# Partial sums written into another PSUM bank by ScalarE, a residual seeded in PSUM, and a reordered start, in a four-block fp16 kernel

## The chip, the cores and the metric

The kernel runs on one core of one Trainium2 chip. The metric is the device time of one execution in microseconds (us), lower is better. A "ratio" below is the mean time of one kernel's fast runs over the mean of the other's fast runs of the same rounds, so it is not quite the ratio of the medians that are quoted beside it.

## The reference, cut to what matters

```python
x = x + A(layernorm(x))   # linear attention, 32 heads of 32, then @ wo
x = x + B(layernorm(x))   # h = (n @ w_gate) * (n @ w_up);  h @ w_down
x = x + A(layernorm(x))
x = x + B(layernorm(x))   # S = 2048 tokens, D = 1024, F = 3584
```

## The kernel before

Every engine has one instruction stream, and a recording helper adds semaphores from the declared reads and writes: `rd`/`wr` for SBUF ranges, `prd`/`pwr` for PSUM banks. The matrix products of block B use a seven-product (Strassen-Winograd) scheme on 2x2 blocks, so a "unit" of gate/up is seven products of four 128x512 matmuls. Gate/up runs four times (two layers, two halves of the tokens), 28 units each; I call each such run a pass. A down stage follows each pass. In the first pass DVE also makes weight combinations that the later passes read back.

The unit of gate/up (cuts marked ...; DVE is VectorE; `stt` is a DVE multiply-add, or with `op1` a multiply, that reads PSUM, `tt` a DVE operation on two inputs; a "product" is one of the seven, `pe("1", ...)` to `pe("7", ...)`):

```python
X, Y, Z = B_GX[u % 2], B_GY[u % 2], B_GZ        # Z: one bank for all units
def cp(i, bank):                                # ScalarE: PSUM -> SBUF
    P.add("act", lambda e: e.activation(tm[i][0], psb(bank), AF.Copy, scale=SG), prd=[bank], wr=tm[i][1])
def fin(b, bank, ti):
    ...
    if ti is None:
        if m == 0:   # gate: ScalarE evicts; up: one DVE multiply
            P.add("act", lambda e: e.activation(g4[b], psb(bank), AF.Copy, scale=SG), prd=[bank], wr=gr)
        else:
            stt(hv[:, j, :], psb(bank), SG, g4[b], gr, hr, prd=[bank], op1=ALU.mult)
    elif m == 0:
        stt(g4[b], psb(bank), SG, tm[ti][0], tm[ti][1], gr, prd=[bank])
    else:            # two DVE operations
        stt(ut, psb(bank), SG, tm[ti][0], tm[ti][1], ur, prd=[bank])
        tt(hv[:, j, :], ut, g4[b], ALU.mult, ur + gr, hr)
def part1():
    pe("1", X, True); cp(0, X)
    pe("2", Z, True); fin(0, Z, 0)
...
# order: 1 2 | 4 of the unit before | 6 | 3 of the unit before | 5 7
```

The end of block A, here the "y stage": sixteen token tiles, two halves each. ScalarE also computes the next layernorm's output in it, and `norm` still runs for two tiles.

```python
def y_grp(i, dh, n):
    ...  # eight matmuls into one of four banks
    if dh == 0:
        P.add("dve", lambda e: e.tensor_tensor(out=xs, in0=psb(bank), in1=xs, op=ALU.add), ...)
        return
    P.add("act", lambda e: e.copy(ysb[yb], psb(bank)), ...)
    P.add("pool", lambda e: e.tensor_tensor(out=xs, in0=xs, in1=ysb[yb], op=ALU.add), ...)
...
O_P = [O_ZACC, RE]                          # buffers of norm
O_YS = [RE + i * 2048 for i in range(2)]    # ysb: the same memory as the second of them
```

The w_down weights are prepared by DVE in 14 "ticks" in the first pass: `if ... wdn[0] * 24 <= u * NJ` with `NJ = 14`. A tick prepares what the tick before it asked to load into a single buffer, and asks for the next.

Of the kernel before, what the change touches and what calls it, by code (L numbers as in the profile page):

```python
# [180 lines left out]
def build_kernel(nc, A_x, A_wqkv, A_wo, B_w_gate, B_w_up, B_w_down, out):  # L181
    _, S, D = A_x.shape
    F = B_w_gate.shape[1]
    NST, NSB, KT, NG, NFT, NDH = S // 128, S // 512, D // 128, D // 128, F // 128, D // 512
    NJ = NFT // 2
# [5 lines left out]
    NHOLD = 2  # L191
# [95 lines left out]
    with ExitStack() as es:  # L287
# [54 lines left out]
        def psb(b):  # L342
            return ps[:, b, :]
# [23 lines left out]
        def R(o, n):  # L367
            return [(o, o + n)]

        def r_x(i, lo=0, hi=D):  # L370
            return [(O_X + (i * D + lo) * 2, O_X + (i * D + hi) * 2)]
# [7 lines left out]
        def r_xT(s0, s1):  # L379
            return _seg(O_XT, KT, S * 2, s0 * 2, s1 * 2)  # L380

        def r_w(base, lo, hi):
            return _seg(base, KT, D * 2, lo * 2, hi * 2)
# [4 lines left out]
        def mset(ap, v, rng):  # L388
            P.add("pool", lambda e: e.memset(ap, v), wr=rng)

        mset(ones, 1.0, R(O_ONES, 256))
        mset(mhalf, -0.5, R(O_MHALF, 4))
        mset(mask, 0.0, R(O_MASK, 256))
# [38 lines left out]
        class LN:  # L432
# [59 lines left out]
            def transpose(self, n):  # L492
                d, r = self.dst(n)
                i = self.order[n]
                if self.use_dma:
                    P.add("sp", lambda e: e.dma_start_transpose(xnT[:, :, i * 128:(i + 1) * 128], d),
                          rd=r, wr=r_xT(i * 128, (i + 1) * 128), dma_sem=KTF[i] if self.to == "A0" else KTL[n % 2])
                    return
                tp = psb_h(B_TP)[:, 0:KT * 128].rearrange("p (k s) -> p k s", s=128)

                def fn(e):
                    return [e.transpose(tp[:, k, :], d[:, k * 128:(k + 1) * 128], ident) for k in range(KT)]
                P.add("pe", fn, rd=r + R(O_IDENT, 256), pwr=[B_TP])
                P.add("act", lambda e: e.copy(xnT[:, :, i * 128:(i + 1) * 128], tp), prd=[B_TP], wr=r_xT(i * 128, (i + 1) * 128))  # L504
# [66 lines left out]
        def ring_issue():  # L571
            n = RG["n"]
            if n >= 2 * NPASS:
                return
            RG["n"] = n + 1
            o = r_slot(n)[0][0]
            ps_, u = divmod(n, NPASS)
            sl = (n + 1) % NR
            if u < NU:
                j, m = divmod(u, 2)  # L580
                raw = vb(o, 2048).rearrange("p (k c) -> p k c", c=256)
                dma(raw, wgu_v[m][:, :, j * 256:(j + 1) * 256], r_slot(n, 0, 4096), KRR[sl])
                if not (RG["first"] and ps_ == 0):
                    dma(vh(o + 4096, 2048), sscr[u], r_slot(n, 4096, 8192), KRS[sl], rd=R(V_S + u * 32, 32))
                return
            q, hf = divmod(u - NU, 2)
            q = DPROD[q]
            js = slice(hf * 7, hf * 7 + 7)
            if q in "123":
                e, d = {"1": (0, 0), "2": (1, 0), "3": (1, 1)}[q]  # L590
                dma(vb(o, 7 * 512).rearrange("p (j c) -> p j c", c=512), wd_v[:, js, e, d * 512:(d + 1) * 512], r_slot(n, 0, 7168), KRR[sl])
            else:
                t = {"5": 0, "6": 1, "7": 2, "4": 3}[q]
                dma(vh(o, 7 * 512).rearrange("p (j c) -> p j c", c=512), tscr[t][:, js, :], r_slot(n, 0, 7168), KRR[sl],
                    rd=R(V_D + hf * 7 * 32, 7 * 32))
# [55 lines left out]
        def layer_A(lnp, nxt, first):  # L651
# [52 lines left out]
            if first:  # L704
                lnp.start(0)
                lnp.b_one()
                lnp.step_t(1)
                lnp.start(1)
                lnp.b_one()
                lnp.start(2)  # L710
            else:
                lnp.use_dma = True
            seq = [("k", i) for i in range(NHOLD)]
            for i in range(NHOLD, NST):
                seq += [("k", i), ("q", i - NHOLD)]
            for kind, i in seq:
                for h in range(2):
                    if kind == "k":
# [96 lines left out]
                wprod(NG + g, [0, 2, 1, 3][g - 4], g % 2 == 0)  # L815
            proj_q(*held[3])()

            def y_grp(i, dh, n):
                bank = B_YY[(2 * n + dh) % 4]

                def fn(e):
                    return [e.matmul(psb(bank), xnT[:, g, i * 128:(i + 1) * 128], wp[:, g, dh * 512:(dh + 1) * 512],  # L822
                                     start=(g == 0), stop=(g == NG - 1)) for g in range(NG)]
                P.add("pe", fn, rd=r_xT(i * 128, (i + 1) * 128) + r_w(O_WP, dh * 512, (dh + 1) * 512), pwr=[bank])
                xs = x_res[:, i, dh * 512:(dh + 1) * 512]
                rx = r_x(i, dh * 512, (dh + 1) * 512)
                if dh == 0:
                    P.add("dve", lambda e: e.tensor_tensor(out=xs, in0=psb(bank), in1=xs, op=ALU.add), prd=[bank], rd=rx, wr=rx)
                    return
                yb = n % 2  # L830
                P.add("act", lambda e: e.copy(ysb[yb], psb(bank)), prd=[bank], wr=R(O_YS[yb], 2048))  # L831
                P.add("pool", lambda e: e.tensor_tensor(out=xs, in0=xs, in1=ysb[yb], op=ALU.add), rd=rx + R(O_YS[yb], 2048), wr=rx)  # L832

            nxt.use_dma = True
            nxt.on_act = YACT
            ring_begin(first)
            for _ in range(3):
                ring_issue()
            for i in range(NST):
                if na[0] < NST:  # L840
                    if i % 3 == 2:
                        norm(tok[na[0]])
                        na[0] += 1
                elif RG["n"] < NR:
                    ring_issue()
                nxt.step_t(1)
                nxt.b1_one()
                if i >= 2:
                    nxt.start(i - 2)
                y_grp(tok[i], 0, i)  # L850
                nxt.b2_one()
                y_grp(tok[i], 1, i)
                if nxt.t_next >= 8 and RG["tq"] is None:
                    RG["tq"] = t_ops(0)
                if RG["tq"]:
                    RG["tq"].pop(0)()
# [3 lines left out]
        def layer_B(lnp, nxt, first):  # L860
# [10 lines left out]
            def unit(ps_, u):  # L871
# [43 lines left out]
                        stt(ut, psb(bank), SG, tm[ti][0], tm[ti][1], ur, prd=[bank])  # L915
                        tt(hv[:, j, :], ut, g4[b], ALU.mult, ur + gr, hr)

                def part1():
                    pe("1", X, True)
                    cp(0, X)  # L920
                    pe("2", Z, True)
                    fin(0, Z, 0)

                def part_p4():
                    pe("4", X, False)
                    fin(2, X, None)

                def part2():
                    pe("6", X, False)
                    cp(1, X)  # L930

# [1 line left out]
                    pe("3", Y, False)  # L933
                    fin(3, Y, 1)

                def part3():
                    pe("5", Y, True)
                    pe("7", X, False)
                    cp(2, X)
                    fin(1, Y, 2)  # L940
                return part1, part_p4, part2, part_p3, part3

            def gateup(ps_, ticks):
                prev = None
                jit = first and ps_ == 0
                for u in range(NU):
                    n = ps_ * NPASS + u
                    cur = unit(ps_, u)
                    if jit and u == 0:
                        prep_s(n)  # L950
                        prep_s(n + 1)
                    cur[0]()
                    if prev:
                        prev[1]()
                    cur[2]()
                    if prev:
                        prev[3]()
                        ring_issue()
                    cur[4]()
                    if jit:  # L960
                        store_s(n)
                        if u + 2 < NU:
                            prep_s(n + 2)
                    ticks(u)
                    prev = cur
                def tail():
                    prev[1]()
                    prev[3]()
                    ring_issue()
                return tail  # L970
# [95 lines left out]
            def ticks0(u):  # L1066
                if not lnp.done():
                    lnp.flush_step()
                if first and wdn[0] < NJ and wdn[0] * 24 <= u * NJ:
                    wd_tick(1)  # L1070
                    wd_tick(0)

# [45 lines left out]
        dh0 = D // 2  # L1118
        dma(x_res[:, 0, 0:dh0], x2[0:128, 0:dh0], r_x(0, 0, dh0), KX[0])
        dma(x_res[:, 0, dh0:D], x2[0:128, dh0:D], r_x(0, dh0, D), KXB)  # L1120
        wq_ = [("k", 0), ("k", 1), ("q", 0), ("q", 1)]
        for i in range(1, NST):
            if wq_ and (i <= NDH or i >= 3):
                load_w(*wq_.pop(0))
            dma(x_res[:, i, :], x2[i * 128:(i + 1) * 128, :], r_x(i), KX[i])

        O_WRM = O_A[0]
        wrm = vh(O_WRM, 512)
        mset(wrm, 0.0, R(O_WRM, 1024))
        P.add("pe", lambda e: [e.matmul(psb(B_KVT[1]), ident, wrm, start=True, stop=True) for _ in range(PE_WARM)],  # L1130
              rd=R(O_IDENT, 256) + R(O_WRM, 1024), pwr=[B_KVT[1]])
        nat = list(range(NST))
        alt = [4, 5, 6, 7, 0, 1, 2, 3, 12, 13, 14, 15, 8, 9, 10, 11]
        lnA = LN("A0", nat)
# [45 lines left out]
```

## Time and profile before

| | before |
|---|---|
| device time, median of 3 | 1507.83 us (1507.47 to 1508.62) |
| TensorE (PE) busy | 98% of the span |
| DVE / ScalarE / GpSimd busy | 65% / 27% / 17% |

The first part of the page gives, for each engine, its busy time, share and number of instructions (PEld is PE's weight loads, ACT ScalarE, POOL GpSimd):

```profile
PE 1481.8 (98%) x6925; PEld 673.9 (45%) x6990; DVE 974.0 (65%) x1642; ACT 400.1 (27%) x643; POOL 257.9 (17%) x271
```

PE is the bound, and its matmuls cannot become fewer in this change. What remains is its idle time. This is PE's own part of the view of waits (who waited for whom: total us, times, longest):

```profile
PE ps L822 <- ACT arena L831: 4.9, 5, 2.1
PE ps L894 <- DVE arena L601: 4.8, 4, 1.6
PE ps L660 <- ACT arena L504: 3.4, 3, 1.1
PE ps L1130 <- POOL arena L389: 3.3, 1, 3.3
PE ps L894 <- DVE arena L598: 1.8, 1, 1.8
...
```

L822 is the y stage, L894 gate/up, L660 the projections, L1130 the warm-up matmuls, L1006 the down stage. The timeline of PE places the waits (start, length, operation, count, and in brackets the idle time before it and who ended it):

```profile
9.19 1.90 PE L660 MATMUL ps<-arena 128*128 128x512 bf16 x8 [1.10 <-ACT arena L504]
11.38 1.90 PE L660 MATMUL ps<-arena 128*128 128x512 bf16 x8 [0.28 <-DMA arena<-in_A_wqkv_dram]
...
20.09 3.63 PE L660 MATMUL ps<-arena 128*128 128x512 bf16 x16 [1.15 <-ACT arena L504]
...
219.15 3.40 PE L822 MATMUL ps<-arena 128*128 128x512 bf16 x15 [1.09 <-ACT arena L831]
...
249.92 15.04 PE L894 MATMUL ps<-arena 128*128 128x512 f16 x68 [1.81 <-DVE arena L598]
266.38 36.43 PE L894 MATMUL ps<-arena 128*128 128x512 f16 x168 [1.42 <-DVE arena L601]
304.23 31.53 PE L894 MATMUL ps<-arena 128*128 128x512 f16 x144 [1.42 <-DVE arena L601]
...
379.29 42.75 PE L894 MATMUL ps<-arena 128*128 128x512 f16 x196 [1.55 <-DVE arena L601]
...
972.19 24.43 PE L822 MATMUL ps<-arena 128*128 128x512 bf16 x102 [2.07 <-ACT arena L831]
```

The rows left out show no other long stall (a second one of 1.15 us in the head, one of 0.36 at 336.13 us, and a few in the y stages). Three passes of gate/up and all down stages have none. So the change can win in the head, in the two y stages (188.08 to 246.22 us and 935.79 to 996.45 us, ScalarE busy 23.47 in each), and in the first pass (246.22 to 422.10 us, DVE busy 143.73).

### The profile page before, as it was taken

To read this page: it belongs to the slowest core of one execution; us is meant where nothing else is said; L and a number is where in the kernel's file an instruction comes from. 1 tells how busy PE (TensorE), PEld (TensorE's weight loads), DVE (VectorE), ACT (ScalarE), POOL (GpSimd) and SP (SyncE) were. 2 spreads that over 40 slices of the span, in tenths; PEclk is the share of its full clock that TensorE was granted. 3 is DMA by queue.
4 is the path that set the end of the run, shared out by engine and by line. 5 is a ranking of instruction groups with operands and counts; after the bars stand their busy time and mean duration, and the time that the engine had idled before them with its cause. 6 is when DMAs were issued, how large, how long until landed. Compare 5 with 4: busy or idle time off the path is not lost.

```text
span 1507.3 us, 17881 instructions
## 1 busy us (share of the span) xinstructions
PE 1481.8 (98%) x6925; PEld 673.9 (45%) x6990; DVE 974.0 (65%) x1642; ACT 400.1 (27%) x643; POOL 257.9 (17%) x271
## 2 busy tenths in 40 slices
PE   8999999999999999999999999999999999999999
PEld 3444444444444444444444444344444444444444
DVE  7986869888856475455488778675455554544553
ACT  3332334333300133330023313343333002333200
POOL 4543644000000010000034345540000000000000
PEclk9999999999999999999999999999999999999999
DMA  6134655988764697644465247656654456555452
GB/s 223 36 91 109 151 125 111 283 262 271 240 224 159 226 257 201 174 162 143 136 195 170 88 102 175 145 120 188 177 172 157 164 189 196 168 176 177 136 172 100
DMA packets 300644, 254.41 MB, mean 169 GB/s; under 512 B 102288, under 2 KB 266384, under 8 KB 300560
## 3 DMA queue, kind: packets, MB, share of 16 engines
q1 hardware_dynamic: 300560, 253.27, 58.4%
q8 instruction: 55, 0.90, 0.3%
q14 instruction: 29, 0.24, 0.0%
HBM read 195.04 MB, written 34.60 MB: 152 GB/s over the span
## 4 chain that ended last, share of the span: by engine, by line
PE 87%; DVE 6%; DMA 3%; POOL 2%; issue 1%; ACT 1%; SPq 0%; POOLq 0%; DVEq 0%; ACTq 0%
PE ps L894 42%; PE ps L1006 22%; PE ps L660 14%; PE ps L741 6%; PE ps L822 2%; DVE arena L598 1%; DMA arena<-arena 1%; DMA arena<-in_B_w_down_dram 1%; DVE arena L408 1%; DVE arena L683 1%; DVE arena L680 1%; POOL arena L689 1%; DMA arena<-in_A_wqkv_dram 1%; DVE arena L601 1%; PE ps L753 0%
## 5 line engine op out<-in xcount | busy, mean ns | idle before, releaser
L894 PE MATMUL ps<-arena 128*128 128x512 f16 x3136 | 679.9, 379 | 6.6 <-DVE arena L601 4.8
L601 DVE SCALAR_TENSOR_TENSOR arena<-ps,arena 128x512 f16<-128x512 f32 (+2 forms) x536 | 364.6, 689 | 415.9 <-PE ps L1006 154.6
L894 PEld LDWEIGHTS ps<-arena 128*128 128x128 f16 (+1 forms) x3136 | 305.4, 98 | 379.8 <-DVE arena L601 9.1
L898 ACT ACTIVATE arena<-ps 128x512 f32<-128x512 f32 x336 | 200.6, 597 | 552.8 <-PE ps L894 549.4
L1006 PE MATMUL ps<-arena 128*128 128x512 f16 (+1 forms) x1548 | 338.0, 379 | 1.1
L1006 PEld LDWEIGHTS ps<-arena 128*128 128x128 f16 x1568 | 153.5, 98 | 185.0
L598 DVE TENSOR_TENSOR arena<-arena 128x512 f16<-128x512 f16 (+3 forms) x416 | 222.7, 557 | 12.2 <-DMA arena<-in_B_w_down_dram 5.0
L660 PE MATMUL ps<-arena 128*128 128x512 bf16 x1003 | 222.4, 379 | 4.8 <-ACT arena L504 3.4
L660 PEld LDWEIGHTS ps<-arena 128*128 128x128 f16 x1024 | 99.6, 98 | 122.7 <-ACT arena L504 3.9
L546 ACT ACTIVATE arena<-ps 128x512 f32<-128x512 f32 x128 | 76.4, 597 | 232.8 <-PE ps L660 217.1
L822 PE MATMUL ps<-arena 128*128 128x512 bf16 x502 | 113.2, 383 | 6.0 <-ACT arena L831 4.9
L411 POOL TENSOR_SCALAR arena<-arena 128x1 f32<-128x1 f32 x64 | 20.7, 324 | 553.3 <-DVE arena L410 553.3
L741 PE MATMUL ps<-arena 128*128 128x512 bf16 x499 | 114.2, 379 | 0.6
L408 DVE BATCH_NORM_STATS2 arena<-arena 128x6 f32<-128x512 bf16 x128 | 88.2, 689 | 8.8 <-DMA arena<-in_A_x_dram 6.6
L549 DVE SCALAR_TENSOR_TENSOR arena<-ps,arena 128x512 bf16<-128x512 f32 x128 | 88.5, 692 | 4.4
L689 POOL TENSOR_TENSOR arena<-arena 128x1024 f16<-128x1024 f32 x32 | 80.2, 2507 | 60.5 <-DVE arena L687 51.0
L672 POOL TENSOR_TENSOR arena<-arena 128x512 f32<-128x512 f32 x60 | 74.6, 1248 | 88.4 <-DVE arena L549 87.0
L547 DVE TENSOR_SCALAR arena<-arena 128x512 f32<-128x512 f32 x128 | 65.6, 513 | 29.5 <-ACT arena L546 28.3
L822 PEld LDWEIGHTS ps<-arena 128*128 128x128 f16 x512 | 49.8, 99 | 69.0 <-ACT arena L831 7.6
L741 PEld LDWEIGHTS ps<-arena 128*128 128x128 f16 x512 | 49.2, 98 | 55.7
L908 ACT ACTIVATE arena<-ps 128x512 f16<-128x512 f32 x56 | 33.4, 597 | 63.3 <-PE ps L894 63.3
L832 POOL TENSOR_TENSOR arena<-arena 128x512 bf16<-128x512 bf16 x32 | 42.1, 1316 | 44.2 <-ACT arena L831 44.2
(41 smaller groups left out, 362.5 us busy)
## 6 DMA issues: line engine op xcount, KB each, us to landing
arena<-s_scratch SPq DMA_DIRECT2D x84, 512.0 KB, 4.4
arena<-in_B_w_gate_dram SPq DMA_DIRECT2D x56, 512.0 KB, 3.9
arena<-in_B_w_up_dram SPq DMA_DIRECT2D x56, 512.0 KB, 4.0
arena<-t_scratch SPq DMA_DIRECT2D x32, 896.0 KB, 4.8
arena<-in_B_w_down_dram SPq DMA_DIRECT2D x24, 896.0 KB, 4.7
s_scratch<-arena SPq DMA_DIRECT2D x28, 512.0 KB, 7.1
arena<-in_A_wqkv_dram SPq DMA_DIRECT2D x12, 1024.0 KB, 8.6
arena<-in_A_x_dram SPq DMA_DIRECT2D x31, 256.0 KB, 4.9
```

Of the source, the lines that this page charges most:

```text
L408: P.add("dve", (lambda h: lambda e: e.bn_stats(st[j][:, 6 * h:6 * h + 6], x_res[:, i, (D // 2) * h:(D // 2) * (h + 1)]))(h), rd=r_x(i, (D ...
L546: P.add("act", lambda e: e.activation(etmp[r], psb(bank), AF.Exp), prd=[bank], wr=er)
L549: P.add("dve", lambda e: e.scalar_tensor_tensor(out=dst_ap, in0=psb(bank), scalar=0.0, in1=etmp[r], op0=ALU.max, op1=ALU.add), prd=[bank], ...
L598: P.add("dve", lambda e: e.tensor_tensor(out=out, in0=a, in1=b, op=op), rd=rd, wr=wr, prd=prd)
L601: P.add("dve", lambda e: e.scalar_tensor_tensor(out=out, in0=a, scalar=sc, in1=b, op0=ALU.mult, op1=op1), rd=rd, wr=wr, prd=prd)
L660: return [e.matmul(psb(bank), xnT[:, k, i * 128:(i + 1) * 128], w[:, k, h * 512:(h + 1) * 512], start=(k == 0), stop=(k == KT - 1)) for k ...
L689: P.add("pool", lambda e: e.tensor_tensor(out=asb[b].rearrange("p (h c) -> p h c", c=32), in0=pbuf.rearrange("p (h c) -> p h c", c=32), in ...
L741: return [e.matmul(psb(bank), xr[:, t, j * 128:(j + 1) * 128], pk[:, h, t, :], start=(t == 0), stop=(t == NST - 1)) for t in range(NST)]
L822: return [e.matmul(psb(bank), xnT[:, g, i * 128:(i + 1) * 128], wp[:, g, dh * 512:(dh + 1) * 512], start=(g == 0), stop=(g == NG - 1)) for ...
L894: P.add("pe", lambda e: [e.matmul(psb(bank), w[:, k, :], x[:, k, :], start=(start and k == 0), stop=(k == 3), skip_group_check=True) for k ...
L898: P.add("act", lambda e: e.activation(tm[i][0], psb(bank), AF.Copy, scale=SG), prd=[bank], wr=tm[i][1])
L1006: return [e.matmul(psb(bank), hv[:, 7 * hf + k, t * 128:(t + 1) * 128], w[:, k, :], start=(start and hf == 0 and k == 0), stop=(hf == 1 an ...
```

## The change

Its intent is to take work off DVE and GpSimd. (a) In gate/up, ScalarE copies product 1 from bank X to bank Z, and product 2 accumulates on top, so that DVE need not add the two. To give the copy time, product 4 of the unit before goes between 1 and 2. (b) The w_down ticks start three units later and follow each other faster. (c) In the y stage, ScalarE puts the residual of the second half into PSUM ahead of the matmuls, and the GpSimd add goes. (d) In the head, the warm-up no longer waits for the identity matrix, the first transpose is evicted in two halves, and query i precedes key i+2. The diff, cut:

```diff
+        P.add("pe", lambda e: [e.matmul(psb(B_KVT[1]), wrm[:, 0:128], wrm, ...) for _ in range(PE_WARM)], ...)   # now first
...
+                if self.to == "A0" and n == 0:     # first transpose in two halves, two copies
...
-                seq += [("k", i), ("q", i - NHOLD)]
+                pair = [("k", i), ("q", i - NHOLD)]
+                seq += pair[::-1] if first and i < NPE_T else pair
...
+            def y_seed(n):
+                    xs, bank = x_res[:, tok[n], 512:1024], B_YY[(2 * n + 1) % 4]
+                    P.add("act", lambda e: e.copy(psb(bank), xs), rd=r_x(tok[n], 512, 1024), pwr=[bank])
...
-                                     start=(g == 0), stop=(g == NG - 1)) for g in range(NG)]
+                                     start=(dh == 0 and g == 0), stop=(g == NG - 1), skip_group_check=True) for g in range(NG)]
...
-                P.add("act", lambda e: e.copy(ysb[yb], psb(bank)), prd=[bank], wr=R(O_YS[yb], 2048))
-                P.add("pool", lambda e: e.tensor_tensor(out=xs, in0=xs, in1=ysb[yb], op=ALU.add), ...)
+                P.add("act", lambda e: e.copy(xs, psb(bank)), prd=[bank], wr=rx)
...
-                def part1():
+                def part_p1():
                     pe("1", X, True)
-                    cp(0, X)
-                    pe("2", Z, True)
-                    fin(0, Z, 0)
+                    P.add("act", lambda e: e.copy(psb(Z), psb(X)), prd=[X], pwr=[Z])
...
+                def part_p26():
+                    pe("2", Z, False)
+                    fin(0, Z, None)
...  # order now: 1 | 4 of the unit before | 2 6 | 3 of the unit before | 5 7; unit 0: 1 5 2 6, 1 of unit 1, 7
-                if first and wdn[0] < NJ and wdn[0] * 24 <= u * NJ:
+                if first and wdn[0] < NJ and wdn[0] * 22 <= (u - 3) * NJ:
```

The rewritten list of first loads issues the same loads in the same order as before.

More of the change, by code (lines that the diff above doesn't have):

```diff
@@ L389, in mset @@
             P.add("pool", lambda e: e.memset(ap, v), wr=rng)
+        wrm = vh(O_A[0], 512)
+        mset(wrm, 0.0, R(O_A[0], 1024))
+        P.add("pe", lambda e: [e.matmul(psb(B_KVT[1]), wrm[:, 0:128], wrm, start=True, stop=True) for _ in range(PE_WARM)],
+              rd=R(O_A[0], 1024), pwr=[B_KVT[1]])
         mset(ones, 1.0, R(O_ONES, 256))
@@ L497, in transpose @@
                           rd=r, wr=r_xT(i * 128, (i + 1) * 128), dma_sem=KTF[i] if self.to == "A0" else KTL[n % 2])
+                    return
+                if self.to == "A0" and n == 0:
+                    for hf, b in enumerate((B_TP, B_KQ[3])):
+                        tq_ = psb_h(b)[:, 0:512].rearrange("p (k s) -> p k s", s=128)
+                        P.add("pe", (lambda hf, tq_: lambda e: [e.transpose(tq_[:, k, :], d[:, (4 * hf + k) * 128:(4 * hf + k + 1) * 128], ident) for k in range(4)])(hf, tq_),
+                              rd=r + R(O_IDENT, 256), pwr=[b])
+                        P.add("act", (lambda hf, tq_: lambda e: e.copy(xnT[:, 4 * hf:4 * hf + 4, i * 128:(i + 1) * 128], tq_))(hf, tq_),
+                              prd=[b], wr=_seg(O_XT + 4 * hf * S * 2, 4, S * 2, i * 256, (i + 1) * 256))
                     return
@@ L706, in layer_A @@
                 lnp.b_one()
+                lnp.start(1)
                 lnp.step_t(1)
-                lnp.start(1)
                 lnp.b_one()
@@ L816, in layer_A @@
             proj_q(*held[3])()
+            def y_seed(n):
+                if n < NST:
+                    xs, bank = x_res[:, tok[n], 512:1024], B_YY[(2 * n + 1) % 4]
+                    P.add("act", lambda e: e.copy(psb(bank), xs), rd=r_x(tok[n], 512, 1024), pwr=[bank])
             def y_grp(i, dh, n):
@@ L822, in fn @@
                     return [e.matmul(psb(bank), xnT[:, g, i * 128:(i + 1) * 128], wp[:, g, dh * 512:(dh + 1) * 512],
-                                     start=(g == 0), stop=(g == NG - 1)) for g in range(NG)]
-                P.add("pe", fn, rd=r_xT(i * 128, (i + 1) * 128) + r_w(O_WP, dh * 512, (dh + 1) * 512), pwr=[bank])
+                                     start=(dh == 0 and g == 0), stop=(g == NG - 1), skip_group_check=True) for g in range(NG)]
                 xs = x_res[:, i, dh * 512:(dh + 1) * 512]
                 rx = r_x(i, dh * 512, (dh + 1) * 512)
+                P.add("pe", fn, rd=r_xT(i * 128, (i + 1) * 128) + r_w(O_WP, dh * 512, (dh + 1) * 512), pwr=[bank])
                 if dh == 0:
@@ L829, in y_grp @@
                     return
-                yb = n % 2
-                P.add("act", lambda e: e.copy(ysb[yb], psb(bank)), prd=[bank], wr=R(O_YS[yb], 2048))
-                P.add("pool", lambda e: e.tensor_tensor(out=xs, in0=xs, in1=ysb[yb], op=ALU.add), rd=rx + R(O_YS[yb], 2048), wr=rx)
+                P.add("act", lambda e: e.copy(xs, psb(bank)), prd=[bank], wr=rx)
             nxt.use_dma = True
@@ L838, in layer_A @@
                 ring_issue()
+            y_seed(0)
             for i in range(NST):
@@ L850, in layer_A @@
                 y_grp(tok[i], 0, i)
+                y_seed(i + 1)
                 nxt.b2_one()
@@ L926, in part_p4 @@
                     fin(2, X, None)
-                def part2():
+                def part_p26():
+                    pe("2", Z, False)
+                    fin(0, Z, None)
                     pe("6", X, False)
@@ L934, in part_p3, with part_p5, part_p7 @@
                     fin(3, Y, 1)
-                def part3():
+                def part_p5():
                     pe("5", Y, True)
+                def part_p7():
                     pe("7", X, False)
@@ L940, in part3 @@
                     fin(1, Y, 2)
-                return part1, part_p4, part2, part_p3, part3
+                return part_p1, part_p4, part_p26, part_p3, part_p5, part_p7
             def gateup(ps_, ticks):
@@ L945, in gateup @@
                 jit = first and ps_ == 0
+                units = [unit(ps_, u) for u in range(NU)]
                 for u in range(NU):
                     n = ps_ * NPASS + u
-                    cur = unit(ps_, u)
+                    cur = units[u]
                     if jit and u == 0:
@@ L951, in gateup @@
                         prep_s(n + 1)
-                    cur[0]()
+                    if u != 1:
+                        cur[0]()
+                    if u == 1:
+                        cur[4]()
                     if prev:
                         prev[1]()
-                    cur[2]()
-                    if prev:
+                        cur[2]()
                         prev[3]()
                         ring_issue()
-                    cur[4]()
+                        if u != 1:
+                            cur[4]()
+                    else:
+                        cur[4]()
+                        cur[2]()
+                        units[1][0]()
+                    cur[5]()
                     if jit:
@@ L1120, in build_kernel, with xload @@
         dma(x_res[:, 0, dh0:D], x2[0:128, dh0:D], r_x(0, dh0, D), KXB)
-        wq_ = [("k", 0), ("k", 1), ("q", 0), ("q", 1)]
-        for i in range(1, NST):
-            if wq_ and (i <= NDH or i >= 3):
-                load_w(*wq_.pop(0))
+        def xload(i):
             dma(x_res[:, i, :], x2[i * 128:(i + 1) * 128, :], r_x(i), KX[i])
-        O_WRM = O_A[0]
-        wrm = vh(O_WRM, 512)
-        mset(wrm, 0.0, R(O_WRM, 1024))
-        P.add("pe", lambda e: [e.matmul(psb(B_KVT[1]), ident, wrm, start=True, stop=True) for _ in range(PE_WARM)],
-              rd=R(O_IDENT, 256) + R(O_WRM, 1024), pwr=[B_KVT[1]])
+        load_w("k", 0)
+        xload(1)
+        load_w("k", 1)
+        xload(2)
+        load_w("q", 0)
+        xload(3)
+        load_w("q", 1)
+        for i in range(4, NST):
+            xload(i)
         nat = list(range(NST))
```

## The prediction

> **What bounds it now.** TensorE. The page gives PE 98% busy. The timeline shows 512-column matmuls 0.216 us apart; the change leaves their number unchanged (112 gate/up units of seven products of four). So only PE idle time can be won. The waits view of PE adds up to about 19 us:
> - head, first 25 us: 3.3 waiting for the warm-up's memset, 1.1 + 1.15 + 1.15 for the ScalarE copy of a transpose, 0.3 for a weight load;
> - residual (y) stages: 2.4 in layer 1, 3.1 in layer 2;
> - first gate/up pass (246-422 us): 6.6. There DVE is busy 144 of 176 us. Three of its five stalls (1.42, 0.36, 1.55) follow a DVE wait for a w_down load;
> - other gate/up and down passes: none.
>
> **Change, costed.**
> 1. *Gate/up.* Per pair of units DVE loses one 0.69 us multiply-add from PSUM and one 0.42 us multiply; ScalarE gains one 0.60 us eviction: about 1.1 us of DVE per 12.1 us pair. Only the first pass has stalls to give. The w_down preparation starts three units later, missing the layernorm work that I blame for the stall at 266 us (1.42). It has five back-to-back ticks against three, but after each the bank that PE needs is one DVE operation away, not two: 0.7 us less per stall. In unit 0, product 5 before 2 costs 0.5 us. Net 6.6 -> about 3.5.
>    New risk: product 2 waits for the copy of product 1 with one product (0.864 us) in between, and product 4 likewise for the eviction of 7. From the trace: ScalarE starts 0.20 us after PE's next issue, 0.585 (a copy) or 0.597 (an activation), 0.055 to PE: 0.84-0.85 us. It just fits; I allow +1 us in all. The Trainium skill, "ScalarE: Activation LUTs"[...], calls PSUM ScalarE's faster destination; this trace has no such copy.
> 2. *y stage.* 32 GpSimd adds of 1.3 us go; 32 seeds of about 0.56 us come on ScalarE, which has room (23.5 of 58 us busy). Half 1 still waits for a layernorm activation two tokens back, now plus a seed. But DVE's wait of 2.0 us for a GpSimd add at 207 us (shared buffer) goes, and what follows comes 2 us earlier. 2.4 + 3.1 -> about 2.3.
>    The seed is added only where the accumulate bits stand: the Trainium skill, "PSUM — Partial Sum Buffer", rule 2, says ScalarE writes leave them, and a matmul without the first flag adds where they are set. Earlier full-bank matmuls set them: I expect correct results.
> 3. *Head.* Warm-up starts at 1.4 us instead of 3.3, but the second key weight half lands at 11.33 us and the load order is unchanged, so that buys nothing. Query 0 before key 2 hides one transpose copy: -1.3 us.
>
> **Sum.** 1507.8 - 1.3 - 3.2 - 3.1 + 1.0 = **1501.2 us**, 8 in 10 between **1496.5 and 1507.5**. Faster by over 2%: 0.01; within: 0.97; slower: 0.02.
>
> **What would show it.** Timeline: second projection still at 11.4 us; no stall before query 0. Waits: GpSimd residual adds gone; y stalls more than halved; first pass stalls 3-4 us. Windows: DVE down about 14 us per gate/up pass, PE unchanged.
>
> **What would make it wrong.** The tight hand-over missing by 0.05 us a unit (+5 us or more); the clock falling back in the idle head (+2 us); more w_down waits reaching PE; or the y stages losing all stalls (-2 us).

## More of the kernel before

The busy times in the first y stage, the first pass, the second y stage, and in one short stretch of the latter (the columns are window, length, busy time of each engine with instruction counts, granted clock, DMA share, GB/s):

```profile
188.08:246.22 58.14, 55.51 (x252) 24.65 (x256) 43.15 (x83) 23.47 (x29) 33.01 (x43) 1.00 0.58 115
246.22:422.10 175.88, 169.23 (x778) 75.07 (x778) 143.73 (x316) 59.20 (x100) 4.21 (x8) 1.00 0.83 248
935.79:996.45 60.66, 57.31 (x252) 25.16 (x256) 42.95 (x83) 23.47 (x29) 33.01 (x43) 0.97 0.64 152
973.40:976.81 3.41, 3.41 (x10) 1.21 (x8) 2.28 (x5) 1.13 (x1) 0.72 (x2) 0.50 0.54 122
```

I did not read the last row before predicting. It matters below: 1.2 us after the end of the stall of 2.07 us (PE goes on at 972.19 us) the clock granted to PE falls to 0.50 for 3.41 us.

## The result, and the profile after

| | before | after |
|---|---|---|
| device time, median of 4 each | 1507.69 us | 1497.39 us (1496.84 to 1497.64) |
| ratio, 95% interval | | 0.993 (0.9913 to 0.9947) |
| span of the trace | 1507.3 us | 1495.1 us |

The outputs are correct, so the matmuls did add to what ScalarE had put into PSUM, as the prediction expected from the page that it names. The time is 3.8 us below the predicted 1501.2 and inside the range. The page's engine line after:

```profile
PE 1479.0 (99%) x6925; PEld 660.1 (44%) x6990; DVE 913.9 (61%) x1530; ACT 449.2 (30%) x732; POOL 216.0 (14%) x239
```

DVE lost 60 us and GpSimd 42, ScalarE gained 49; the number of matmuls is the same. PE's waits after (L840 is the y stage, L912 gate/up, L672 the projections, L938 the copy between banks, L834 the seed):

```profile
PE ps L840 <- ACT ps L834: 2.7, 3, 1.4
PE ps L672 <- DMA arena<-in_A_wqkv_dram: 1.6, 1, 1.6
PE ps L393 <- POOL arena L389: 1.4, 1, 1.4
PE ps L912 <- DVE arena L613: 1.3, 2, 0.9
...
PE ps L912 <- ACT ps L938: 0.6, 1, 0.6
...
```

And the timeline of PE after:

```profile
7.91 1.90 PE L672 MATMUL ps<-arena 128*128 128x512 bf16 x8 [0.74 <-ACT arena L508]
11.41 1.90 PE L672 MATMUL ps<-arena 128*128 128x512 bf16 x8 [1.60 <-DMA arena<-in_A_wqkv_dram]
...
18.82 7.07 PE L672 MATMUL ps<-arena 128*128 128x512 bf16 x32
...
220.69 22.62 PE L840 MATMUL ps<-arena 128*128 128x512 bf16 x102 [0.92 <-ACT ps L834]
243.15 77.12 PE L912 MATMUL ps<-arena 128*128 128x512 f16 x356
320.62 48.78 PE L912 MATMUL ps<-arena 128*128 128x512 f16 x224 [0.35 <-DVE arena L613]
370.33 42.48 PE L912 MATMUL ps<-arena 128*128 128x512 f16 x196 [0.93 <-DVE arena L613]
...
960.75 3.63 PE L840 MATMUL ps<-arena 128*128 128x512 bf16 x16 [1.44 <-ACT ps L834]
```

The second projection starts at 11.41 us as before (11.38): the warm-up starts earlier, and PE then waits for a weight load. The first pass starts with no stall and has two small ones. The windows of the same three stages:

```profile
186.80:243.15 56.35, 55.16 (x253) 24.96 (x257) 44.25 (x86) 33.78 (x45) 14.04 (x29) 1.00 0.58 122
243.15:412.86 169.71, 168.29 (x777) 72.12 (x777) 127.53 (x285) 66.11 (x113) 2.33 (x6) 1.00 0.83 254
926.35:983.68 57.33, 55.33 (x252) 24.87 (x256) 42.42 (x82) 32.14 (x44) 14.01 (x28) 1.00 0.62 160
```

From one stage's first matmul to the next stage's, the traces differ by: projections -1.3 us, first y stage -1.8, first pass -6.2, second y stage -3.3, the pass after it +0.6 (a new wait for the copy), the rest -0.2. The sum is -12.2 us, the difference of the two spans. The medians differ by less, 10.3 us, and the fall of the clock is most of the reason. Of 27 runs of the kernel before, 17 have a mean granted clock of 1.000 (median 1507.25 us) and ten one of 0.998 or 0.999 (1507.96 to 1511.10 us). The profiled run of the kernel before is one of the latter kind (0.999, 1509.03 us): its second y stage shows some 1.7 us that most runs, and so the median, do not have.

Two rows of the traces explain more than the rest. First, the start of the first pass in the kernel before, where PE waited 1.81 us (timeline of all engines in a window of 1.2 us):

```profile
248.34 1.16 POOL L832 TENSOR_TENSOR arena<-arena 128x512 bf16<-128x512 bf16 x1
248.34 1.43 DVE L598 TENSOR_TENSOR arena<-arena 128x512 f16<-128x512 f16 x1
```

The DVE operation is the second of eight that prepare the first two units, and product 6 of the first needs its result. It took 1.43 us; its seven neighbours took 0.41 to 0.43 us. A GpSimd residual add ran from the same moment for 1.16 us. The Trainium skill, "SBUF — State Buffer", section "Who interferes with whom", says that a DVE instruction with two SBUF inputs contends with a GpSimd instruction that reads SBUF, that the shared port pair is an exclusive lock, and that the issue order decides who blocks. The trace agrees, roughly: waiting out 1.16 us and then a normal 0.42 would be 1.6, and 1.43 were seen. The opposite order is in the same trace, where the DVE operation came first and the add took 1.79 us:

```profile
237.72 1.22 DVE L598 TENSOR_TENSOR arena<-arena 128x2048 f16<-128x2048 f16 x1
238.17 1.79 POOL L832 TENSOR_TENSOR arena<-arena 128x512 bf16<-128x512 bf16 x1
```

So it was with all eight of the 32 adds that began while such a DVE operation on two SBUF inputs ran (1.74 to 1.79 us). The other 24 took 1.16 or 1.17, also those that ran beside DVE operations with only one input in SBUF.

Second, the wait inside the first y stage of the kernel before (timeline; L680 is `norm` on the second buffer, which shares its memory with `ysb`):

```profile
206.21 1.16 POOL L832 TENSOR_TENSOR arena<-arena 128x512 bf16<-128x512 bf16 x1 [0.38 <-ACT arena L831]
207.41 1.23 DVE L680 TENSOR_TENSOR arena<-arena 128x1024 f32<-128x1024 bf16 x1 [1.98 <-POOL arena L832]
```

### The profile page after: what moved, and what is told of

It is laid out like the page before. It is cut to its first block, busy times and chain, and to the rows that moved or that the text cites. A ratio compares the mean times of both kernels' runs of the same rounds, so it can differ in the third digit from the quotient of the medians.

```text
span 1495.1 us, 17704 instructions
## 1 busy us (share of the span) xinstructions
PE 1479.0 (99%) x6925; PEld 660.1 (44%) x6990; DVE 913.9 (61%) x1530; ACT 449.2 (30%) x732; POOL 216.0 (14%) x239
## 3 DMA queue, kind: packets, MB, share of 16 engines
q1 hardware_dynamic: 300560, 253.27, 57.4%
## 4 chain that ended last, share of the span: by engine, by line
PE 91%; DVE 3%; DMA 3%; issue 1%; POOL 1%; ACT 1%; SPq 0%; ACTq 0%
PE ps L912 43%; PE ps L1035 23%; PE ps L672 15%; PE ps L754 7%; PE ps L840 2%; DMA arena<-in_B_w_down_dram 1%; DVE arena L610 1%; DVE arena L412 1%; DMA arena<-arena 1%; DMA arena<-in_A_wqkv_dram 1%; POOL arena L701 1%; PE ps L766 0%; PE ps L794 0%; SPq L386 0%; POOL arena L417 0%
## 5 line engine op out<-in xcount | busy, mean ns | idle before, releaser
L912 PE MATMUL ps<-arena 128*128 128x512 f16 x3136 | 679.0, 379 | 1.9 <-DVE arena L613 1.3
L613 DVE SCALAR_TENSOR_TENSOR arena<-ps,arena 128x512 f16<-128x512 f32 (+2 forms) x480 | 327.2, 689 | 470.6 <-PE ps L912 161.8
L912 PEld LDWEIGHTS ps<-arena 128*128 128x128 f16 (+1 forms) x3136 | 291.4, 98 | 388.2 <-ACT arena L916 36.0
L672 PE MATMUL ps<-arena 128*128 128x512 bf16 x1003 | 222.1, 379 | 4.6 <-DMA arena<-in_A_wqkv_dram 1.6
L916 ACT ACTIVATE arena<-ps 128x512 f32<-128x512 f32 x224 | 133.7, 597 | 291.1 <-PE ps L912 288.9
L610 DVE TENSOR_TENSOR arena<-arena 128x512 f16<-128x512 f16 (+3 forms) x360 | 197.9, 574 | 18.3 <-DMA arena<-in_B_w_down_dram 8.3
L672 PEld LDWEIGHTS ps<-arena 128*128 128x128 f16 x1024 | 99.6, 98 | 122.4 <-DMA arena<-in_A_wqkv_dram 2.1
L558 ACT ACTIVATE arena<-ps 128x512 f32<-128x512 f32 x128 | 76.4, 597 | 232.6 <-PE ps L672 218.4
L938 ACT COPY ps<-ps 128x512 f32<-128x512 f32 x112 | 63.9, 570 | 204.3 <-PE ps L912 203.7
L840 PE MATMUL ps<-arena 128*128 128x512 bf16 x502 | 110.8, 379 | 3.2 <-ACT ps L834 2.7
L926 ACT ACTIVATE arena<-ps 128x512 f16<-128x512 f32 x112 | 66.9, 597 | 84.5 <-PE ps L912 84.5
L840 PEld LDWEIGHTS ps<-arena 128*128 128x128 f16 x512 | 49.8, 98 | 63.9 <-ACT ps L834 4.4
L754 PEld LDWEIGHTS ps<-arena 128*128 128x128 f16 x512 | 49.3, 98 | 55.7
```

The source lines that it names most:

```text
L558: P.add("act", lambda e: e.activation(etmp[r], psb(bank), AF.Exp), prd=[bank], wr=er)
L610: P.add("dve", lambda e: e.tensor_tensor(out=out, in0=a, in1=b, op=op), rd=rd, wr=wr, prd=prd)
L613: P.add("dve", lambda e: e.scalar_tensor_tensor(out=out, in0=a, scalar=sc, in1=b, op0=ALU.mult, op1=op1), rd=rd, wr=wr, prd=prd)
L672: return [e.matmul(psb(bank), xnT[:, k, i * 128:(i + 1) * 128], w[:, k, h * 512:(h + 1) * 512], start=(k == 0), stop=(k == KT - 1)) for k ...
L754: return [e.matmul(psb(bank), xr[:, t, j * 128:(j + 1) * 128], pk[:, h, t, :], start=(t == 0), stop=(t == NST - 1)) for t in range(NST)]
L840: return [e.matmul(psb(bank), xnT[:, g, i * 128:(i + 1) * 128], wp[:, g, dh * 512:(dh + 1) * 512], start=(dh == 0 and g == 0), stop=(g == ...
```

## The experiments

Twelve kernels ran. All outputs were correct. The median of the kernel before was 1508.12, 1507.84 and 1507.41 us in the three calls; the changed kernel did not run in them, so I compare with its ratio, 0.993, and with its trace. Times by stage from the traces (first matmul to the next stage's first matmul, the projections from the start of the span; us; one trace each):

| kernel | projections | y stage 1 | first pass | y stage 2 | median, ratio (95%) |
|---|---|---|---|---|---|
| before | 118.1 | 58.1 | 175.9 | 60.7 | |
| after | 116.9 | 56.4 | 169.7 | 57.3 | 1497.39, 0.9930 (0.9913-0.9947) |
| e1_head | 117.0 | 57.7 | 174.7 | 63.1 | 1506.63, 0.9988 (0.9976-1.0001) |
| e2_y | 117.6 | 56.3 | 173.8 | 59.1 | 1502.69, 0.9961 (0.9949-0.9974) |
| e3_gu | 118.2 | 57.8 | 172.0 | 60.5 | 1502.97, 0.9965 (0.9953-0.9978) |
| e4_ysb | 117.7 | 55.8 | 174.6 | 58.8 | 1503.46, 0.9965 (0.9952-0.9979) |
| e5_oldtick | 116.2 | 56.7 | 171.9 | 57.4 | 1498.07, 0.9933 (0.9920-0.9945) |
| e6_p1sbuf | 117.0 | 56.5 | 170.2 | 58.9 | 1498.20, 0.9937 (0.9924-0.9949) |
| e7_adjacent | 116.3 | 57.0 | 189.4 | 58.9 | 1582.69, 1.0496 (1.0481-1.0510) |
| e8_spaced | 116.6 | 56.4 | 169.8 | 57.7 | 1496.49, 0.9923 (0.9910-0.9937) |
| e9_yorder | | | | | 1494.48 (3 fast runs), 0.9909 (0.9894-0.9925) |
| e10_headT | 115.5 | 57.0 | 170.2 | 57.5 | 1496.08, 0.9920 (0.9906-0.9933) |
| e11_latewarm | 116.8 | 56.6 | 170.3 | 57.3 | 1496.69, 0.9923 (0.9911-0.9935) |
| e12_best | 115.4 | 55.3 | 169.3 | 55.7 | 1492.79, 0.9898 (0.9885-0.9912) |

Stages that are the same code differ between traces by up to 2.6 us in the second y stage (60.5 in e3_gu, 63.1 in e1_head), 1.2 in the first pass (174.6 in e4_ysb, 175.9 before) and 0.8 in the others. A difference of one trace below that is not an argument by itself.

### e1_head: only the start

The kernel before with the hunks of the diff that concern the head, and nothing else.

> Only the head of the change (early warm-up, first transpose in two halves, query 0 before key 2). My theory: the second key weight half still lands at 11.3 us, so the early warm-up gives nothing, and one hidden transpose copy gives 1.3 us: the stage after the projections starts 1.3 us earlier (116.85 us), all later stages as before, 1506.4 us. Rival: the 1.9 us that the warm-up starts earlier are won too: 3 us or more.

The projections are 1.2 us shorter in the trace, as expected, and the second projection waits 1.6 us for its weights. The time ratio does not exclude 1 (0.9976 to 1.0001). Two of the five runs have a clock of 0.998, the profiled one among them: there a stall of 3.7 us in the second y stage was followed by 6.8 us at half clock. Among runs with a clock of 1.000, the median is 1506.20 us of three, against 1507.67 of five of the kernel before. The rival (3 us or more) is excluded for the stage, less firmly for the time.

### e2_y: only the y stage

The kernel before with `y_seed` and the new `y_grp`.

> Only the y stage of the change (seed in PSUM, no GpSimd add). My theory: 1.8 us from the first y stage and about 2.7 from the second; and, because in the kernel before a GpSimd add ran at the same time as the second of the eight preparation operations of DVE at the start of the first gate/up pass (1.43 us in place of 0.42), that operation takes 0.42 us here and the first gate/up stall falls from 1.8 us to under 0.5. Sum -5 to -6.5 us, about 1502. Rival: the stall at the start of gate/up belongs to the order of the products, and stays at 1.8: -4.5 at most.

-1.9 and -1.6 us in the y stages, -2.1 in the first pass, median 1502.69: as expected in sum. In the first pass the GpSimd add is gone, and the same preparation operation now merges with the next in the timeline, two in 0.76 us:

```profile
245.63 0.76 DVE L598 TENSOR_TENSOR arena<-arena 128x512 f16<-128x512 f16 x2
```

The stall at the start, with the old order of products, is the one before this row of PE:

```profile
246.20 15.03 PE L899 MATMUL ps<-arena 128*128 128x512 f16 x68 [0.33 <-DVE arena L598]
```

It fell from 1.81 to 0.33 us. The rival falls. The second y stage is another matter: its stalls are 1.92 and 1.54 us, more than the 3.1 before, and no half clock followed them. In this trace the seed did not shorten them; the 1.6 us are about what the half clock had cost.

### e3_gu: only gate/up

The kernel before with the copy between banks, the new order and the new ticks.

> Only the gate/up part of the change (product 1 copied between PSUM banks, order, later w_down ticks). My theory: y stages unchanged (5.5 us of stalls), the slow preparation operation of 1.43 us is still there, the later first-pass stalls fall from 4.8 to about 1.3; first pass about 3.5 to 4.5 us shorter, about 1503.7 us. No stall per unit: the matmuls of the other passes stay 0.216 us apart. Rival: the whole 6.2 us of the first pass come from this part alone, with the start stall gone.

The first pass is 3.9 us shorter; its preparation operation still took 1.44 us beside a GpSimd add, and a stall of 1.27 us was left at its start:

```profile
248.20 59.86 PE L894 MATMUL ps<-arena 128*128 128x512 f16 x276 [1.27 <-DVE arena L598]
```

The two parts add up: -2.1 (e2_y) and -3.9 give -6.0, and the whole change has -6.2. The sum is looser than it looks, since the same first pass took 174.6 to 175.9 us in three traces. What holds is the stall: 1.80 or 1.81 us in those three traces, 0.33 without the adds. So some 1.5 us of what the first pass won, about a quarter, came from the y stage's GpSimd adds. My theory of this run holds.

### e4_ysb: the buffer moved, nothing else

```diff
-    O_YS = [RE + i * 2048 for i in range(2)]
+    O_YS = [O_DOUT + i * 2048 for i in range(2)]
```

> The kernel before, with the ScalarE-to-GpSimd staging buffers of the y stage moved away from the second norm buffer that they share memory with; nothing else. My theory of the y stages: DVE's 2.0 us wait for a GpSimd add at 207 us, and ScalarE's 0.8 us wait for a GpSimd multiply, are due to this sharing, so most of the y gain comes with the move alone: y stalls 5.5 -> 2 to 3.5 us, 1504.5 us. Rival: the gain needs the GpSimd adds to go (they delay the small layernorm operations behind them): less than 1 us.

The first y stage has no stall left and is shorter than in the changed kernel (55.8 against 56.4 us), and the stall at the start of the first pass is untouched, as this timeline of PE shows:

```profile
188.08 55.97 PE L822 MATMUL ps<-arena 128*128 128x512 bf16 x251
243.88 1.89 PE L894 MATMUL ps<-arena 128*128 128x512 f16 x8
247.57 15.03 PE L894 MATMUL ps<-arena 128*128 128x512 f16 x68 [1.80 <-DVE arena L598]
```

Sharing memory between `ysb` and the norm buffer was the cause of the stalls in the first y stage. The seed in PSUM needs no `ysb` either, but has a wait of its own: 0.92 us behind a seed is left in the changed kernel. In the second y stage a stall of 3.1 us remained in this trace, so the move is no cure there; that stage is shorter (58.8 against 60.7 us) because no half clock followed.

### e5_oldtick: the old w_down schedule

```diff
-wdn[0] * 22 <= (u - 3) * NJ
+wdn[0] * 24 <= u * NJ
```

> The changed kernel with the old w_down schedule. My theory: the stall near the third unit, where layernorm and w_down preparation meet, comes back, and three waits for w_down remain: first gate/up pass 0.5 to 1.5 us longer, 1498.4 us. Rival: the schedule does not matter, or the old one is better since it has three back-to-back ticks against five: same or 1 us shorter.

The first pass is 2.2 us longer in the trace, with stalls of 0.68 and 0.56 us at 256 and 261 us, where layernorm work and w_down work meet, and 1.00, 0.19 and 0.74 later. In time it is not told apart from the changed kernel: 0.9933 against 0.9930. The stall came back where I thought; its worth in time stays open (2.2 us in the one trace, 0.7 between medians).

### e6_p1sbuf: product 1 through SBUF again

```diff
-                    P.add("act", lambda e: e.copy(psb(Z), psb(X)), prd=[X], pwr=[Z])
+                    cp(0, X)
...
-                    pe("2", Z, False)
-                    fin(0, Z, None)
+                    pe("2", Z, True)
+                    fin(0, Z, 0)
```

> The changed kernel, its order kept, but product 1 evicted to SBUF and added on DVE as before. If the 14 us of DVE work per pass matter in the first pass, as I think, its stalls go from 1.3 to 3 to 5 us: 1499 to 1501 us; the other passes do not change. Rival: order and schedule alone made the gain: no change.

A miss. DVE has its work back (window of the first pass):

```profile
243.90:414.10 170.20, 168.17 (x778) 73.61 (x778) 140.62 (x313) 58.56 (x99) 2.15 (x5) 1.00 0.84 253
```

140.6 us of DVE against 127.5, and the pass is only 0.5 us longer; its stalls are 0.41, 0.96 and 0.60 us. The time, 0.9937 (0.9924 to 0.9949), overlaps that of the changed kernel; the medians differ by 0.8 us. So the copy into another PSUM bank, which the change is named after, is not shown to be worth anything here: 0.5 us in the trace, 0.8 in time, both within the noise. By elimination the order of the products, the tick schedule and the missing GpSimd add made the gain of the first pass; no run changes the order alone.

### e7_adjacent: product 2 directly behind product 1

```diff
                     if prev:
+                        cur[2]()
                         prev[1]()
-                        cur[2]()
```

> The changed kernel with product 2 directly behind product 1 in units 2 to 27 of each pass. My reading of the hand-over (0.20 us to ScalarE, 0.57 for the copy, 0.055 back) says that PE waits 0.8 us in each of 104 units: +83 us, about 1580. Rival: PE's queue or the copy's overlap hides a part: under +50.

+85 us. Each pass takes 189.43 us in place of 167.70, or 0.836 us for each of 26 units. Every time PE waits for the copy (an idle time of 0.66 counts from the modelled end of the matmul before):

```profile
702.78 5.35 PE L912 MATMUL ps<-arena 128*128 128x512 f16 x24 [0.66 <-ACT ps L938]
```

So the copy's hand-over (from PE to ScalarE and back) costs 0.84 us when it is exposed, and the one product of 0.864 us that the change puts in between hides all of it. In the changed kernel the same hand-over reads like this (timeline; PEld is the weight load in front of a product's matmuls, released by ScalarE):

```profile
1303.20 0.60 ACT L916 ACTIVATE arena<-ps 128x512 f32<-128x512 f32 x1 [1.99 <-PE ps L912]
1303.43 1.89 PE L912 MATMUL ps<-arena 128*128 128x512 f16 x8
...
1303.85 0.55 PEld L912 LDWEIGHTS ps<-arena 128*128 128x128 bf16 x4 [0.32 <-ACT arena L916]
1304.06 0.57 ACT L938 COPY ps<-ps 128x512 f32<-128x512 f32 x1 [0.27 <-PE ps L912]
1304.68 0.36 PEld L912 LDWEIGHTS ps<-arena 128*128 128x128 bf16 x3 [0.29 <-ACT ps L938]
```

The weight loads are held back by ScalarE, PE's matmuls are not: over 1250 to 1400 us all matmul starts are 0.215 or 0.216 us apart (where no record is missing).

### e8_spaced: no two ticks in a row

```diff
-wdn[0] * 22 <= (u - 3) * NJ
+2 * wdn[0] + 1 <= u
```

> The changed kernel with the w_down ticks at every second unit (1, 3 ... 27), so that no tick follows another. A load takes about 6 us from issue to landing and a unit 6.05 us, so only back-to-back ticks make DVE wait: DVE waits for w_down fall from 8.3 us to under 1 and the stalls of 0.35 and 0.93 us go: -1.2 us, 1496.2 us. Rival: the last ticks delay the loads of their results in the down stage: no gain or a new stall.

Half a miss. DVE's waits for w_down are gone (8.3 us in five waits in the changed kernel), and so are the two stalls; but a tick in unit 1 meets the layernorm again, and a stall like that of the kernel before (1.42 us at 266.38) is back:

```profile
244.25 15.71 PE L912 MATMUL ps<-arena 128*128 128x512 f16 x72 [0.30 <-DVE arena L610]
261.38 151.26 PE L912 MATMUL ps<-arena 128*128 128x512 f16 x700 [1.41 <-DVE arena L613]
```

The first pass stays at 169.8 us. In 151 us after that there is no stall, so a schedule that starts at unit 3 and has no two ticks in a row should win both (not tried); there are 13 such places for 14 ticks.

### e9_yorder: layernorm transposes ahead of norm in the DMA queue

```diff
             for i in range(NST):
+                nxt.step_t(1)
                 if na[0] < NST:
                     ...
-                nxt.step_t(1)
```

> The changed kernel with the layernorm transpose issued ahead of the norm (and ahead of the weight load) in each turn of the y loop. In the changed kernel a layernorm transpose that could go at 203.2 us went at 210.1, behind the norm's reload and transpose in the one DMA queue, and the ScalarE activation that waits for its buffer held up the seeds. My theory: the y stalls (0.92 in layer 1, 1.74 + 0.57 around layer 2) shrink to under 1 us in all: -2 to -3 us, 1495 us. Rival: the stalls come from ScalarE's own load (34 of 58 us): under 0.5 us.

Three fast runs of 1493.76 to 1495.10 us, ratio 0.9909: their median is 2.9 us below the changed kernel's, as expected, though the two intervals overlap (0.9894 to 0.9925 against 0.9913 to 0.9947). The profiled execution fell into a slow state of 3204.54 us, in which most 512-column matmuls were 0.44 or 0.56 us apart, while DVE and ScalarE operations took what they take elsewhere (0.597 us for an activation). Its trace holds no clock record at all, so the clock of 1.00 that the query gives is no reading. I did not see this in any other run, do not explain it, and use nothing of that trace. The y stages of this edit are seen in e12_best.

### e10_headT: transposes between halves of projections

```diff
-                else:
+                    if i == 0:
+                        lnp.step_t(1)      # transpose 1 after the first half of key 0
+                elif i >= 2:
...
+                        if first and i == 0 and h == 0:
+                            lnp.step_t(1)  # transpose 2 after the first half of query 0
```

> The changed kernel with transpose 1 between the two halves of key 0 and transpose 2 between the halves of query 0. The copy of transpose 1 then hides behind a projection: the stall of 1.15 us at 13.7 us goes, nothing else: -1.05 us, 1496.3 us. Rival: the head is bound by the arrival of the weights, so it is the same.

The projections take 115.5 us, 1.35 less than in the changed kernel; in the six other traces with the changed kernel's head or nearly so (e5_oldtick to e8_spaced, e1_head, e11_latewarm) they take 116.2 to 117.0. The median is 1496.08, not told apart from the changed kernel's. The rival, that weights bind the head, falls by the traces.

### e11_latewarm: the warm-up where it was

The changed kernel without the early warm-up and without the split of the first transpose.

> The changed kernel with the warm-up where it was before and the first transpose whole; query 0 stays before key 2. My theory: no change (the second key half at 11.33 us bounds both), within 0.4 us of 1497.4. Rival: the early warm-up is worth its 1.9 us: 1499.3.

1496.69 us, and 116.8 us of projections against 116.9. The early warm-up and the split together are worth nothing that shows, as the arrival of the second key half said.

### e12_best: the three amendments together

> All three amendments (spaced ticks, transposes first in the y loop, transposes between halves in the head) on the changed kernel. If each gain is a PE stall of its own stage they add: -4 to -5 us, about 1493 us.

1492.79 us, ratio 0.9898 (0.9885 to 0.9912): faster than both kernels, and 4.6 us below the changed one's median. The y stages take 55.3 and 55.7 us; 256 matmuls at 0.2158 us are 55.2. Of the y stalls 0.3 us are left, in the second stage, but the wait for a copy at the start of the pass behind it, 0.57 us in the changed kernel, is now 0.99: together 1.3, a little more than e9_yorder expected. PE's largest waits that are left:

```profile
PE ps L916 <- DVE arena L613: 1.4, 1, 1.4
PE ps L393 <- POOL arena L389: 1.4, 1, 1.4
...
PE ps L916 <- ACT ps L942: 1.0, 1, 1.0
...
```

## Why the prediction was right or wrong, point by point

- **Bound: right.** Only PE's idle time was won (and in the profiled pair 1.7 us of half clock); the matmuls kept their number, and of the three passes without stalls two kept their time (167.70 us before and after), the third lost 0.6.
- **Head, -1.3 us: right**, -1.3 in the trace, with the mechanism shown by e1_head and e11_latewarm.
- **y stages, "2.4 + 3.1 -> about 2.3": mechanism right for the first (e4_ysb), not for the second.** Stalls that remain are 0.9 and 1.7 us, and 0.6 at the start of the pass behind them, a little more than predicted. In the second stage the stalls sum to 3.1 to 4.7 us in three traces of the old y stage, 3.2 with `ysb` moved (e4_ysb), 1.7 to 3.5 in eight traces with the seed, and 0.3 with the transposes first in the DMA queue (e12_best, one trace): there the order in that queue counts for more than the shared buffer. Still the second stage became 3.3 us shorter in the profiled pair, where its stalls shrank by 1.4: in the kernel before, the clock fell to half for 3.41 us after the longest stall, and matmuls 0.427 us apart in place of 0.216 cost some 1.7 us. That term was missing. A y stage that stalls long enough pays twice, but only some runs do (ten of 27 by their mean clock), so the median has little of it. Without it the two stages won some 3.4 us against 3.2 predicted: close, and for the second stage by luck.
- **First pass, "Net 6.6 -> about 3.5": the term that failed.** Its stalls fell to 1.3. The failing term is "In unit 0, product 5 before 2 costs 0.5 us", which kept the start stall of 1.81 and added to it. I had taken the slow DVE stretch at the start for plain DVE work. It was one operation held up by a GpSimd add. With the adds gone the stall is 0.33 (e2_y), with the new order alone 1.27 (e3_gu: the order made it shorter, not longer), with both 0. The mis-sized term, 1.81 + 0.5, is 2.3 us of the 3.8 by which the prediction was too high.
- **DVE relieved of 14 us per pass: right as a size** (143.7 -> 127.5 us of the first pass), **but it was not what mattered**: with that work back, the pass is 0.5 us longer (e6_p1sbuf), which is within the noise. "One DVE operation away, not two" comes from the order of products 4 and 2, which e6_p1sbuf keeps.
- **Hand-over, +1 us: wrong by its size.** In the changed kernel's trace nothing is lost to it in the first pass, nor in the second and fourth (167.70 us each); in the third (168.45 us) one copy came 0.57 us late behind the y stage's own ScalarE work. In the first pass of four other traces with the copy (e3_gu, e5_oldtick, e10_headT, e11_latewarm) PE waited for it for 0.2 to 0.9 us in all. The estimate of 0.84 to 0.85 us was right: e7_adjacent gives 0.836 when it is exposed. I should have trusted it.
- **PSUM as ScalarE's faster destination:** the Trainium skill, "ScalarE: Activation LUTs", section Step-by-step: what each stage is for, is borne out, but by little: the copy between banks takes 0.570 us, the copies from PSUM to SBUF in the kernel before took 0.585 when ScalarE had been idle. The seeds, which go from SBUF to PSUM, took 0.589 and not the 0.56 of the prediction.

Open: what the copy between banks is worth in time (0.8 us between medians, not told apart from nothing), what the tick schedule alone is worth (0.7 us likewise), and what the order of the products alone is worth.

## What to carry to other kernels

When the bound engine is 98% busy, list its stalls one by one and find for each the single operation that was late; totals of engine work say little (some 15 us of DVE per pass were worth 0.5 in the one trace). Look for two buffers that share memory, and for a GpSimd operation that starts together with a slow DVE one, before rebuilding the arithmetic: a one-line move of a buffer won nearly as much as the whole y-stage rewrite. A hand-over to another engine and back was free here when something a little longer stood between: 0.84 us hidden behind 0.864, and 85 us lost when nothing did. And compare runs by their granted clock before reading a difference of 2 us.

## What the Trainium skill lacked or had wrong

- "TensorE: Matmul & The Clock Gate", section What's actually happening, has the clock fall after at least one idle window of about 3.4 us, and the section on oscillation asks for no idle gap over about 3.4 us. Here shorter gaps were enough: 2.2 us of idle PE in one window of 3.413 us brought half clock for 3.41 us (kernel before, 973.4 us; e3_gu, 968.4 us), and in e1_head 2.3 us of a window, of a gap of 3.8 us, brought 6.83 us. In the head of e12_best and e6_p1sbuf two gaps that sum to 2.2 and 2.5 us in one window did the same. 2.1 us in one window (e2_y) did not, nor a gap of 3.2 us that two windows shared at 1.8 and 1.4 (e4_ysb). Idle times count from one issue slot (0.216 us, 0.06 for a transpose) after the last matmul's start; windows are counted in steps of 3.413 us from the first clock record. Five falls and a few near misses (the next is 2.0, in e8_spaced) are not many. The page's section on a second failure mode does tell of short idle times that did it, but without a length.
- "SBUF — State Buffer", section Who interferes with whom, names the contention, with slowdowns of 6.8 and 1.5 times, but gives no duration or size for this pair: a DVE operation of 0.42 us took 1.43 to 1.44 us beside a GpSimd add of 1.16 us in four kernels (before, e1_head, e3_gu, e4_ysb), and 0.42 or 0.43 in nine other traces, without the add; an add issued after a DVE operation of 1.22 us took 1.79. A GpSimd operation on 128x1 elements (0.57 us) beside a DVE operation did not lengthen it (0.42).
- No page that I read has the time of a ScalarE copy from one PSUM bank to another: 0.570 us for 128x512 fp32, and 0.84 us for PE to ScalarE and back around it.
- No page that I read describes an execution like that of e9_yorder, with most 512-column matmuls 0.44 or 0.56 us apart over 3200 us, the other engines' operations as long as ever, and no clock record in the trace.
